# A change of the tile order of batches 0 and 1, of where late weights are decoded, and of how sign and low word are merged

## The chip, the core and the metric

One core of a Trainium2 chip runs the whole program in one launch. The metric is the device time of an execution in microseconds. Before the change three runs took 1471.87 to 1477.98 us, with a median of 1476.96 us.

## What is computed

Attention through 32 packed rows, then a gated layer, then a bilinear one, all in float32:

```python
p_packed = sm_attn(p, k, v)                # 8 batches, 8 heads, 576 rows of 64; 32 packed rows
out = sm_attn(q, p_packed, p_packed)
x = out.transpose(0, 2, 1, 3).reshape(4608, 512)
h = x @ w_in                               # 512 -> 2048
x = (h / (1 + exp(-h))) @ w_out            # 2048 -> 512
out = ((x @ w1) * (x @ w2)) @ w3 @ wo2     # 512 -> 1024 -> 1024 -> 512
```

The weights reach the kernel as float64 words, which it turns into float32 on the chip.

## The kernel before, in words

A matmul of two float32 operands is made of three fp32r matmuls (`mm3`, lines 94 to 97): each operand is split into a high part and a rest (`split`, lines 79, 83 and 88), and high times high, rest times high and high times rest are summed in PSUM.

**Decoding weights.** A float64 tile of 128 x 512 (512 KB) becomes float32 in `Decode` (line 157). ScalarE scales the high words and the low words (line 171 and the one before); VectorE shifts the high word left by three (line 173); the low word is added by GpSimd and the sign bit merged in by VectorE. Without a PSUM bank the add comes first and the merge takes its result (lines 176 and 177); with one, where the high word lies in PSUM, the merge goes into the low word first (line 182) and the add comes last (line 186).

**Stage 1** runs 256 tiles. A tile is one half (f) of a batch (b), 288 rows, and one block m of 128 of the 2048 columns. `emit_h` makes h from a2[b] (the attention weights) and a gate tile of one of 8 slots; `emit_g` applies tanh on ScalarE (line 838) and the product gg on VectorE (line 843), and splits gg on ScalarE and GpSimd; `emit_x2`, three tiles later, multiplies by wo[m] into four PSUM banks, which are evicted to x2_d in DRAM when the last m of the pass is in. The order of the tiles is the list `items`: batch 0 passes half 0 with m 0 to 7, half 1 with m 0 to 7, half 1 with m 8 to 15, half 0 with m 15 to 8, and the first sum of half 0 is stored and added at the end (line 869). From batch 1 on a half passes all 16 m at once. `fetch` (line 781) fills the slots up to 16 tiles ahead from m_d or m01_d, a DMA and a split each.

**The start.** `START` (line 68) is an order written out by hand: what stands before the first bar is emitted ahead of the tiles, and what stands up to the next bar behind each tile. F is a fill, that is a decode of one of 32 tiles of w_in and w_out (order: w_in 0 to 7, w_out 0 to 7, w_in 8 to 15, w_out 8 to 15); L asks for the next raw tile ahead; T is `direct`, a matmul of packed rows of batches 0 and 1 by a w_in tile; W stores a w_in tile to wi_d for later batches; P0, P1, S0, S1 are steps of attention units of batch 0 and 1. Before the change 9 fills stand ahead of the tiles, 7 on tiles 0 to 3, and 16 on tiles 4 to 17; the 16 T stand on tiles 4 to 12 and the 16 W on tiles 6 to 16.

**Three streams** run beside the tiles, paced by `over`, `pack_in` and `paces` (a range of tiles each over which their steps come due, lines 1019 to 1048). Stream x: attention units, one after the other (`chain`): Pack (softmax of the packed rows), four for two batches, and Spread (softmax of the rows, ends with a2), two a batch; the Spreads of batch 1 are due over tiles 15 to 20, the Packs of batches 2 and 3 over 26 to 38, the Spreads of batch 2 over 44 to 62; from tile 209 `prepare_second`, 47 steps due by tile 250, which makes the weights of stage 2: sums of w1 and w2 tiles (`combine`), and the product of w3 and wo2 (`turn`, `product`). Stream y: PackIn, packed rows by w_in for two batches, over 44 to 66. Stream z: `decode_late`, which decodes the 40 tiles of wo2, w3, w1 and w2 over tiles 70 to 205 and stores them to late_d (256 KB each); `prepare_second` reads them back. A planner orders each engine's instructions from this emission order with times of its own.

**Stage 2** (line 1163 on) runs 36 steps of three-part matmuls by the prepared weights.

Of the kernel before, what the change touches and what calls it, by code (L numbers as in the profile page):

```python
# [8 lines left out]
F32 = mybir.dt.float32  # L9
F32R = mybir.dt.float32r  # L10
I32 = mybir.dt.int32
# [11 lines left out]
def attention_swiglu_chain(  # L23
# [39 lines left out]
    EXTRA = 24  # L63
# [69 lines left out]
    late_d = [dram.tile([128, 512], F32, name=f"late_d{n}") for n in range(5 * KM2)]  # L133
# [19 lines left out]
    def bank(name):  # L153
        return ps_f.tile([128, 512], F32, tag="f", name=name)


    class Decode:
# [7 lines left out]
        def __init__(self, raw, z, ps=None):  # L165
            def word(dtype, t):
                return raw.bitcast(dtype).rearrange("p (n t) -> p n t", t=2)[:, :, t]

            high = word(F32, 1) if ps is None else ps
            act_copy(high, word(F32, 1), 2.0**-112)  # L170
            act_copy(word(I32, 0), word(U32, 0), 2.0**-29)
            high = high.bitcast(I32)
            V.tensor_scalar(out=z, in0=high, scalar1=3, scalar2=None, op0=ALU.logical_shift_left)
            if ps is None:
                low = word(I32, 0)
                G.tensor_tensor(out=z, in0=z, in1=low, op=ALU.add)
                V.scalar_tensor_tensor(
                    out=z, in0=high, scalar=-(2**31), in1=z, op0=ALU.bitwise_and, op1=ALU.bitwise_or
                )
            else:  # L180

                V.scalar_tensor_tensor(  # L182
                    out=word(I32, 0), in0=high, scalar=-(2**31), in1=word(I32, 0),
                    op0=ALU.bitwise_and, op1=ALU.bitwise_or,
                )
                G.tensor_tensor(out=z, in0=z, in1=word(I32, 0), op=ALU.add)
            self.z = z.bitcast(F32)
# [109 lines left out]
    class Rows:  # L297
# [6 lines left out]
        def load_rows(self, src):  # L304
            self.x = {}
            src = src[self.b, self.hg]
            for f in self.halves:
                hs = slice(f * HS, (f + 1) * HS)
                if self.early:
                    tag = "gg" if self.lane.second else "sg"  # L310
                    self.x[f] = []
                    for e in range(2):
                        t = g_p.tile([128, HS], F32, tag=tag, name="qT", bufs=2)
# [396 lines left out]
    used_up = [4, 5, 6, 7, 0, 1, 2, 3]  # L710
# [63 lines left out]
    items = [(b, f, m) for b, f in halves[2:] for m in (range(KM) if f == 0 else range(KM - 1, -1, -1))]  # L774

    early_m, late_m = range(KM // 2), range(KM // 2, KM)
    items = [(0, f, m) for f, ms in ((0, early_m), (1, early_m), (1, late_m), (0, late_m[::-1])) for m in ms] + items
    split_at = KM // 2
# [42 lines left out]
    came = []  # L821
    gt = {}
# [13 lines left out]
    def emit_g(i, ps):  # L836
# [5 lines left out]
        gg = g_p.tile([128, HS], F32, tag="gg", name="gg", bufs=2)  # L842
# [7 lines left out]
    def emit_x2(i):  # L850
# [3 lines left out]
        if first_m:  # L854
            acc[b, f] = [ps_acc.tile([128, 512], F32, tag=f"acc{c}", name="ps_x2")[:, 0:HS] for c in range(CD)]
        h_, l_ = gt.pop(i)
        assert ("o", m) in ready
        w = wo[m]
# [3 lines left out]
        if last_m:  # L862
            xs = g_p.tile([128, CD, HS], F32, tag="xs", name="xs", bufs=1)
            rest = (b, f) == (0, 0) and i >= split_at
            if rest:
                move(out=xs, in_=x2_d[b, f])
# [24 lines left out]
    def decode_late():  # L891


        def raw():
            return at.tile([128, 512], U64, tag="raw2", name="raw2", bufs=3)
# [13 lines left out]
        load()  # L909
        yield  # L910
        for n in range(len(late)):
            if n + 2 < len(late):
                load()
            with tc.issue_after(behind["sg"]):
                z = Decode(raws[n], room(n)).z
            store(out=late_d[n], in_=z, age=1)
            yield

    def prepare_second():

        attn.close()
        with tc.tile_pool(name="dec2", bufs=1, side="right") as dp:
            zs = []

            def load():
                n = len(zs)
                zs.append(dp.tile([128, 512], F32, tag="z", name="z", bufs=12))
                move(out=zs[n], in_=late_d[n])
# [49 lines left out]
            ps_w = bank("ps_w34")  # L978
# [48 lines left out]
    over(15, 20, plain([Spread(1, 0), Spread(1, 1)]))  # L1027
# [12 lines left out]
    paces["z"].append((70, at0 + 13, len(late) + 1))  # L1040
# [288 lines left out]
```

## Time and profile before

| what | value |
|---|---|
| median of 3 runs | 1476.96 us |
| the profiled execution's own time | 1475.26 us |
| its span, first to last instruction | 1473.5 us |
| mean granted TensorE clock | 0.987 of full |
| busy: TensorE, its weight loads | 1404.5 us (95%), 1312.4 us (89%) |
| busy: VectorE, ScalarE, GpSimd | 926.1 us (63%), 662.6 us (45%), 601.0 us (41%) |
| moved by DMA | 215.75 MB, mean 146 GB/s |

The span is the time between the first and the last instruction of the profiled execution; its own time is a little longer. Tile 0's tanh stands at 49.5 us, the last tile's at 900.6 us, and stage 2 takes the rest. TensorE is called busy when any matmul is in flight, so the number of matmuls that pass in a stretch tells more than its busy share. A mean over the span mixes stages with different limits; the rows below are by stretch.

### The profile page before, as it was taken

To read this page: it belongs to the slowest core of one execution; us is meant where nothing else is said; L and a number is where in the kernel's file an instruction comes from. 1 tells how busy PE (TensorE), PEld (TensorE's weight loads), DVE (VectorE), ACT (ScalarE), POOL (GpSimd) and SP (SyncE) were. 2 spreads that over 40 slices of the span, in tenths; PEclk is the share of its full clock that TensorE was granted. 3 is DMA by queue.
4 is the path that set the end of the run, shared out by engine and by line. 5 is a ranking of instruction groups with operands and counts; after the bars stand their busy time and mean duration, and the time that the engine had idled before them with its cause. 6 is when DMAs were issued, how large, how long until landed. Compare 5 with 4: busy or idle time off the path is not lost. (4 is left out here: it accounts for less than half of the span.)

```text
span 1473.5 us, 26073 instructions
## 1 busy us (share of the span) xinstructions
PE 1404.5 (95%) x9548; PEld 1312.4 (89%) x9548; DVE 926.1 (63%) x1743; ACT 662.6 (45%) x1442; POOL 601.0 (41%) x606
## 2 busy tenths in 40 slices
PE   7779999799899999999999999999999999999998
PEld 5558999689899998899998899999999999999997
DVE  5976857557876669886888525345454545545453
ACT  5766555556567565575455433223232222323221
POOL 2779655677769966779554231000000000000000
PEclk9999999899999999999999999999999999999999
DMA  8489523676568755476499518610110101101000
GB/s 302 152 276 309 180 82 108 202 227 185 173 182 260 226 174 165 151 235 194 144 303 308 185 63 327 275 58 3 56 49 10 58 1 58 34 25 58 1 30 29
DMA packets 151360, 215.75 MB, mean 146 GB/s; under 512 B 15808, under 2 KB 103104, under 8 KB 150208
## 3 DMA queue, kind: packets, MB, share of 16 engines
q1 hardware_dynamic: 130240, 188.92, 39.8%
q10 hardware_dynamic: 20992, 25.17, 4.9%
q8 instruction: 75, 1.23, 0.3%
q14 instruction: 53, 0.43, 0.1%
HBM read 144.24 MB, written 69.80 MB: 145 GB/s over the span
## 5 line engine op out<-in xcount | busy, mean ns | idle before, releaser
L95 PE MATMUL ps_x<-gh,wo 128*128 128x288 f32 x1024 | 300.8, 298 | 4.0 <-DVE raw L182 3.1
L96 PE MATMUL ps_x<-gh,wo 128*128 128x288 f32 x1024 | 301.4, 298 | 0.0
L97 PE MATMUL ps_x<-gl,wo 128*128 128x288 f32 x1024 | 284.7, 300 | 3.7 <-POOL gl L88 3.3
L88 POOL TENSOR_TENSOR gl<-gg,gh 128x288 fp32r<-128x288 f32 x256 | 232.0, 908 | 94.8 <-ACT gh L79 85.9
L1170 PE MATMUL ps_ab<-xct,w 128*128 128x256 f32 x1728 | 221.2, 284 | 0.0
L1170 PEld LDWEIGHTS ps_ab<-xct,w 128*128 128x128 f32 x1728 | 214.9, 190 | 1.0
L88 POOL TENSOR_TENSOR mq<-mr,mq 128x256 fp32r<-128x256 f32 x176 | 148.9, 847 | 133.5 <-DVE mq L83 68.5
L95 PEld LDWEIGHTS ps_x<-gh,wo 128*128 128x128 f32 x1024 | 193.3, 189 | 7.7 <-DVE raw L182 3.3
L96 PEld LDWEIGHTS ps_x<-gh,wo 128*128 128x128 f32 x1024 | 193.3, 189 | 2.1 <-issue 1.4
L97 PEld LDWEIGHTS ps_x<-gl,wo 128*128 128x128 f32 x1024 | 186.1, 189 | 9.4 <-POOL gl L88 6.4
L79 ACT ACTIVATE gh<-gg 128x288 fp32r<-128x288 f32 x256 | 112.9, 443 | 178.7 <-DVE gg L843 172.3
L95 PE MATMUL ps_h<-a,mq 128*128 128x288 f32 x512 | 159.7, 312 | 24.4 <-DVE gg L843 18.8
L1170 PE MATMUL ps_ab<-xcb,w 128*128 128x256 f32 x1296 | 176.2, 283 | 2.6 <-issue 2.6
L1187 DVE TENSOR_TENSOR r<-p,ps_ab 128x512 f32<-128x512 f32 x72 | 49.2, 684 | 204.0 <-PE ps_ab L1170 203.9
L1170 PEld LDWEIGHTS ps_ab<-xcb,w 128*128 128x128 f32 x1296 | 167.6, 189 | 6.9 <-issue 2.8
L843 DVE SCALAR_TENSOR_TENSOR gg<-sg,ps_h 128x288 f32<-128x288 f32 x256 | 114.0, 446 | 82.4 <-ACT sg L838 37.0
L97 PE MATMUL ps_h<-a,mq 128*128 128x288 f32 x512 | 153.4, 300 | 0.5 <-DVE a L88 0.4
L96 PE MATMUL ps_h<-a,mq 128*128 128x288 f32 x512 | 153.2, 299 | 0.0
L95 PEld LDWEIGHTS ps_h<-a,mq 128*128 128x128 f32 x512 | 97.9, 191 | 37.5 <-DVE gg L843 27.2
L838 ACT ACTIVATE sg<-ps_h 128x288 f32<-128x288 f32 x256 | 102.3, 403 | 56.0 <-PE ps_h L97 31.0
L97 PE MATMUL ps_o<-w,abh 128*128 128x512 f32 x280 | 109.6, 391 | 0.0
L96 PE MATMUL ps_o<-w,abl 128*128 128x512 f32 x280 | 109.5, 391 | 0.0
(177 smaller groups left out, 2582.7 us busy)
## 6 DMA issues: line engine op xcount, KB each, us to landing
mr<-m_d SPq DMA_DIRECT2D x144, 128.0 KB, 3.3
raw<-in_moe_w_dram SPq DMA_DIRECT2D x32, 512.0 KB, 4.4
w_d<-w12s ACTq DMA_DIRECT2D x56, 256.0 KB, 3.9
w<-w_d SPq DMA_DIRECT2D x8, 1792.0 KB, 14.8
wz<-wi_d SPq DMA_DIRECT2D x48, 256.0 KB, 3.8
m_d<-ms SPq DMA_DIRECT2D x96, 128.0 KB, 3.2
raw<-in_moe_w_out_dram SPq DMA_DIRECT2D x21, 512.0 KB, 4.5
late_d<-z ACTq DMA_DIRECT2D x40, 256.0 KB, 4.4
```

Of the source, the lines that this page charges most:

```text
L79: A.activation(out=dst, in_=src, func=ACTF.Copy, scale=mul)
L88: (eng or V).tensor_tensor(out=lo, in0=src, in1=hi.bitcast(F32), op=ALU.subtract)
L95: T.matmul(out=dst, lhsT=wh, rhs=xh, start=start, stop=False)
L96: T.matmul(out=dst, lhsT=wl, rhs=xh, start=False, stop=False)
L97: T.matmul(out=dst, lhsT=wh, rhs=xl, start=False, stop=stop)
L838: ins = A.activation(out=sg, in_=ps, func=ACTF.Tanh, scale=0.5)
L843: ins = V.scalar_tensor_tensor(out=gg, in0=sg, scalar=1.0, in1=ps, op0=ALU.add, op1=ALU.mult)
L1170: T.matmul(out=bank[:, x], lhsT=w[:, wp], rhs=xt[:, kt, xp], start=first and (x, kt, n) == (0, 0, 0), stop=last and (x, kt, n) == (1, 1, 2 ...
L1187: V.tensor_tensor(out=dst, in0=p, in1=q, op=op)
```

## The change

Five things change. The `items` list lets the four halves of batches 0 and 1 pass m 0 to 7, then the four halves pass m 8 to 15; each half's first sum is stored, and loaded again when four tiles of its second pass are in (`part_x2`), where it is added on VectorE. The plan `START` and the due ranges follow: the last 16 fills stand on tiles 8 to 34, eight T on tiles 3 to 6 and eight on tiles 16 to 23, the W on tiles 7 to 10 and 24 to 27; the Spreads of batch 1 are due over tiles 5 to 14; `used_up` takes the tiles in their natural order, and the two raw buffers that lie in a2's place are used by the first 15 fills, not 24. Stream z decodes 20 late tiles (`MID`) over the same tiles 70 to 205; the other 20 are loaded raw and decoded in `prepare_second`, with the high word in a PSUM bank, `ps_dec`. Every decode merges the sign into the low word and adds on GpSimd last. Buffers: gg 4 for 2, raw2 2 for 3, z of `prepare_second` 6 for 12, with three tiles asked for ahead in place of six.

```diff
-    EXTRA = 24
+    EXTRA = 15
+    MID = 20
...
-        "| F F S1 | F S1 | F F S1 | F F | F F T T | F F T T | F W W | F T T W W | F F T T | W W T T "
-        "| F W W T T | F T T | F T T | F W W | F W W | F W W | F W W | F S0 S1 |"
+        "| F L F L S1 | F L S1 | F F S1 | F F T T | T T | T T | T T L | W W L | F L W W | W W | F L W W | | F L "
+        "| | F L | | F T T | T T | F L | | F L | | F T T | T T | W W | L W W | F L W W | W W "
+        "| F L | F L | F L | F L | F L | F L | F | S0 S1 |"
...
-            if ps is None:
-                low = word(I32, 0)
-                G.tensor_tensor(out=z, in0=z, in1=low, op=ALU.add)
-                V.scalar_tensor_tensor(
-                    out=z, in0=high, scalar=-(2**31), in1=z, op0=ALU.bitwise_and, op1=ALU.bitwise_or
-                )
-            else:
...
+            V.scalar_tensor_tensor(
+                out=word(I32, 0), in0=high, scalar=-(2**31), in1=word(I32, 0),
+                op0=ALU.bitwise_and, op1=ALU.bitwise_or,
+            )
+            G.tensor_tensor(out=z, in0=z, in1=word(I32, 0), op=ALU.add)
...
-    used_up = [4, 5, 6, 7, 0, 1, 2, 3]
+    used_up = [0, 1, 2, 3, 4, 5, 6, 7]
...
-    items = [(0, f, m) for f, ms in ((0, early_m), (1, early_m), (1, late_m), (0, late_m[::-1])) for m in ms] + items
-    split_at = KM // 2
+    items = [(b, f, m) for h in range(2) for b, f in halves[:4] for m in range(h * KM // 2, (h + 1) * KM // 2)]
+    items += [(b, f, m) for b, f in halves[4:] for m in (range(KM) if f == 0 else range(KM - 1, -1, -1))]
...
+        rest = (b, f) in part_x2
+        if rest and i == passes[0] + 4:
+            part_x2[b, f] = g_p.tile([128, CD, HS], F32, tag="xs", name="xs", bufs=1)
+            move(out=part_x2[b, f], in_=x2_d[b, f])
...
-            return at.tile([128, 512], U64, tag="raw2", name="raw2", bufs=3)
+            return at.tile([128, 512], U64, tag="raw2", name="raw2", bufs=2)
...
-        for n in range(len(late)):
-            if n + 2 < len(late):
+        for n in range(MID):
+            if n + 1 < MID:
                 load()
...
+            ps_dec, ps_w = bank("ps_dec"), bank("ps_w34")
...
-                zs.append(dp.tile([128, 512], F32, tag="z", name="z", bufs=12))
-                move(out=zs[n], in_=late_d[n])
+                if n < MID:
+                    zs.append(dp.tile([128, 512], F32, tag="z", name="z", bufs=6))
+                    move(out=zs[n], in_=late_d[n])
+                else:
+                    zs.append(dp.tile([128, 512], U64, tag="raw", name="raw", bufs=3))
+                    DMA.dma_start(out=zs[n], in_=late_srcs[n])
...
-                while len(zs) < min(n + 6, len(late)):
+                while len(zs) < min(n + 3, len(late)):
                     load()
                 (kind, i), z = late[n], zs[n]
+                if n >= MID:
+                    z = Decode(z, dp.tile([128, 512], I32, tag="z", name="z", bufs=6), ps_dec).z
...
-    over(15, 20, plain([Spread(1, 0), Spread(1, 1)]))
+    over(5, 14, plain([Spread(1, 0), Spread(1, 1)]))
...
-    paces["z"].append((70, at0 + 13, len(late) + 1))
+    paces["z"].append((70, at0 + 13, MID + 1))
```

## Rows read from the trace of the kernel before

**Rows 1.** Table of stretches: us, busy (x instructions) by engine, clock, DMA share, GB/s.

```profile
63.40:120.60 57.20, 46.83 (x256) 37.44 (x256) 46.71 (x59) 36.40 (x75) 48.38 (x40) 0.93 0.74 246
120.60:183.50 62.90, 61.60 (x426) 57.40 (x425) 48.51 (x93) 36.28 (x84) 50.16 (x53) 1.00 0.74 237
183.50:264.90 81.40, 81.40 (x608) 80.23 (x607) 51.28 (x132) 46.93 (x116) 48.92 (x53) 1.00 0.36 107
264.90:288.70 23.80, 15.14 (x78) 12.02 (x77) 13.14 (x19) 10.09 (x20) 12.66 (x12) 0.87 0.66 194
288.70:725.00 436.30, 418.04 (x2991) 404.50 (x2991) 333.24 (x660) 259.70 (x603) 340.20 (x336) 0.99 0.62 192
725.00:831.00 106.00, 101.48 (x670) 94.06 (x668) 84.57 (x178) 54.06 (x138) 49.41 (x56) 1.00 0.90 293
831.00:886.00 55.00, 54.59 (x341) 50.61 (x342) 15.97 (x36) 18.85 (x43) 17.67 (x23) 1.00 0.20 74
```

**Rows 2.** Stretches again, line 838 alone (tanh on ScalarE, one a tile).

```profile
63.40:120.60 57.20, 4.83 (x12) 0.93 0.74 246
120.60:183.50 62.90, 7.81 (x20) 1.00 0.74 237
```

**Rows 3.** Waits of TensorE in 49.5 to 183.5 us: total, times, longest.

```profile
PE ps_m L668 <- DVE zi L177: 5.5, 1, 5.5
```

**Rows 4.** Timeline, single instructions of the attention units, 163 to 287 us.

```profile
163.83 0.76 DVE L587 STREAM_TRANSPOSE sT<-s 128x576 f32<-128x576 f32 x1
...
167.75 0.38 PE L438 MATMUL ps_t<-ident,e 128*128 128x128 f32 x2
...
235.11 0.38 PE L438 MATMUL ps_t<-ident,e 128*128 128x128 f32 x2
...
284.52 0.78 DVE L587 STREAM_TRANSPOSE sT<-s 128x576 f32<-128x576 f32 x1
...
286.68 0.61 PE L95 MATMUL ps_h<-a,mq 128*128 128x288 f32 x1 [1.29 <-ACT a L79]
```

**Rows 5.** Waits of SP's queue in 215 to 292 us.

```profile
SPq L105 <- POOL v L88: 20.3, 2, 11.7
```

**Rows 6.** Lines 177, 182, 176, 173: ns min/median/max, first and last start; VectorE's wait.

```profile
L177 DVE SCALAR_TENSOR_TENSOR z<-raw,z x49: 680/1277/1785, 72.1 to 720.7; 128x512 int32<-128x512 int32 x49
...
  POOL z L176: 24.8, 20
...
L182 DVE SCALAR_TENSOR_TENSOR raw<-ps_dec,raw x8: 654/679/692, 21.9 to 61.2; 128x512 int32<-128x512 int32 x8
...
L176 POOL TENSOR_TENSOR z<-z,raw x49: 1290/1312/1946, 64.6 to 719.4; 128x512 int32<-128x512 int32 x49
...
L173 DVE TENSOR_SCALAR z<-raw x49: 407/427/1522, 61.8 to 718.6; 128x512 int32<-128x512 int32 x49
...
L173 DVE TENSOR_SCALAR z<-ps_dec x6: 678/680/691, 44.5 to 60.6; 128x512 int32<-128x512 int32 x6
```

**Rows 7.** Waits of TensorE in 288.7 to 725 us.

```profile
PE ps_h L95 <- DVE gg L843: 14.9, 13, 3.6
```

**Rows 8.** DMA issues: count, KB each, median us from issue to landing.

```profile
raw<-in_moe_w_dram SPq DMA_DIRECT2D x32, 512.0 KB, 4.4
...
z<-late_d SPq DMA_DIRECT2D x40, 256.0 KB, 4.5
...
xs<-x_d SPq DMA_DIRECT2D x1, 576.0 KB, 6.3
```

**Rows 9.** Line 869, the adding eviction.

```profile
L869 DVE SCALAR_TENSOR_TENSOR xs<-ps_x,xs x4: 420/452/458, 176.4 to 180.7; 128x288 f32<-128x288 f32 x4
```

**Rows 10.** Tiles late_d and w3T: reloads, and the split of w3T.

```profile
L105 SPq DMA_DIRECT2D z<-late_d x40: 319/332/1179, 726.5 to 808.6; - x40
...
L88 DVE TENSOR_TENSOR w3T<-z,w3T x16: 673/682/1226, 739.1 to 861.7; 128x512 fp32r<-128x512 f32 x16
```

More of the change, by code (lines that the diff above doesn't have):

```diff
@@ L132, in attention_swiglu_chain @@
     w34_d = [dram.tile([128, 2, 512], F32, name=f"w34_d{i}") for i in range(KM2)]
-    late_d = [dram.tile([128, 512], F32, name=f"late_d{n}") for n in range(5 * KM2)]
+    late_d = [dram.tile([128, 512], F32, name=f"late_d{n}") for n in range(MID)]
     x2_d = {(b, f): dram.tile([128, CD, HS], F32, name=f"x2_d{b}_{f}") for b in range(B) for f in range(2)}
@@ L173, in __init__ @@
             V.tensor_scalar(out=z, in0=high, scalar1=3, scalar2=None, op0=ALU.logical_shift_left)
-            if ps is None:
-                low = word(I32, 0)
-                G.tensor_tensor(out=z, in0=z, in1=low, op=ALU.add)
-                V.scalar_tensor_tensor(
-                    out=z, in0=high, scalar=-(2**31), in1=z, op0=ALU.bitwise_and, op1=ALU.bitwise_or
-                )
-            else:
[L182 to L186, printed above, removed]
+            V.scalar_tensor_tensor(
[3 more added lines that the diff above has]
+            G.tensor_tensor(out=z, in0=z, in1=word(I32, 0), op=ALU.add)
             self.z = z.bitcast(F32)
@@ L312, in load_rows @@
                     for e in range(2):
-                        t = g_p.tile([128, HS], F32, tag=tag, name="qT", bufs=2)
+                        t = g_p.tile([128, HS], F32, tag=tag, name="qT", bufs=4 if self.lane.second else 2)
                         move(out=t, in_=src[:, e, hs])
@@ L773, in attention_swiglu_chain @@
     halves = [(b, f) for b in range(B) for f in range(2)]
-    items = [(b, f, m) for b, f in halves[2:] for m in (range(KM) if f == 0 else range(KM - 1, -1, -1))]
-    early_m, late_m = range(KM // 2), range(KM // 2, KM)
-    items = [(0, f, m) for f, ms in ((0, early_m), (1, early_m), (1, late_m), (0, late_m[::-1])) for m in ms] + items
-    split_at = KM // 2
+    items = [(b, f, m) for h in range(2) for b, f in halves[:4] for m in range(h * KM // 2, (h + 1) * KM // 2)]
+    items += [(b, f, m) for b, f in halves[4:] for m in (range(KM) if f == 0 else range(KM - 1, -1, -1))]
     uses = [(b, m) for b, f, m in items]
@@ L821, in attention_swiglu_chain @@
     came = []
+    passes, part_x2 = [0], {}
     gt = {}
@@ L841, in emit_g @@
         behind["sg"] = ins.ins
-        gg = g_p.tile([128, HS], F32, tag="gg", name="gg", bufs=2)
+        gg = g_p.tile([128, HS], F32, tag="gg", name="gg", bufs=4)
         ins = V.scalar_tensor_tensor(out=gg, in0=sg, scalar=1.0, in1=ps, op0=ALU.add, op1=ALU.mult)
@@ L855, in emit_x2 @@
             acc[b, f] = [ps_acc.tile([128, 512], F32, tag=f"acc{c}", name="ps_x2")[:, 0:HS] for c in range(CD)]
+            passes[0] = i
         h_, l_ = gt.pop(i)
         assert ("o", m) in ready
+        rest = (b, f) in part_x2
+        if rest and i == passes[0] + 4:
+            part_x2[b, f] = g_p.tile([128, CD, HS], F32, tag="xs", name="xs", bufs=1)
+            move(out=part_x2[b, f], in_=x2_d[b, f])
         w = wo[m]
@@ L862, in emit_x2 @@
         if last_m:
-            xs = g_p.tile([128, CD, HS], F32, tag="xs", name="xs", bufs=1)
-            rest = (b, f) == (0, 0) and i >= split_at
             if rest:
-                move(out=xs, in_=x2_d[b, f])
+                xs = part_x2.pop((b, f))
+            else:
+                xs = g_p.tile([128, CD, HS], F32, tag="xs", name="xs", bufs=1)
+                if b < 2:
+                    part_x2[b, f] = None
             for c in range(CD):
@@ L908, in decode_late @@
         load()
-        load()
         yield
-        for n in range(len(late)):
-            if n + 2 < len(late):
+        for n in range(MID):
+            if n + 1 < MID:
                 load()
@@ L923, in prepare_second @@
             zs = []
+            ps_dec, ps_w = bank("ps_dec"), bank("ps_w34")
             def load():
                 n = len(zs)
[L927 to L928 removed]
+                if n < MID:
+                    zs.append(dp.tile([128, 512], F32, tag="z", name="z", bufs=6))
+                    move(out=zs[n], in_=late_d[n])
+                else:
+                    zs.append(dp.tile([128, 512], U64, tag="raw", name="raw", bufs=3))
+                    DMA.dma_start(out=zs[n], in_=late_srcs[n])
             o = [dp.tile([128, 2, 512], F32R, name=f"wo2_{j}") for j in range(KM2)]
@@ L976, in step @@
                         combine(i // 2)
-            ps_w = bank("ps_w34")
             w3T = {}
```

## The prediction, made before the changed kernel was run

> **What bounds the kernel now.** I read the table of stretches first: the reader is to see how many matmuls each stretch passes and what the other engines do meanwhile. TensorE is "busy" nearly everywhere, so the count per microsecond is the better gauge. From 183.5 to 264.9 us 608 matmuls pass in 81.4 us, 0.134 us each, with TensorE never idle [rows 1]; I take that as its full pace in the first stage. Against it, 63.4 to 120.6 us holds 256 matmuls, 34.3 us of work in 57.2 us; 120.6 to 183.5 us holds 426, 57.1 us in 62.9 us; 264.9 to 288.7 us holds 78, 10.5 us in 23.8 us [rows 1]. From 831 to 886 us TensorE is busy 54.6 of 55 us [rows 1]: little is left there. So the time to be won lies in 63.4 to 183.5 us (28.7 us), in the hole at 264.9 us (13.3 us) and, thinly spread, in 288.7 to 725 us, where 2991 matmuls (400.8 us) take 436.3 us. The 0.134 us is short for the 512-column and the four-byte matmuls among them, so the true losses are some us smaller.
>
> The count of sigmoid instructions, one a tile, dates the tiles: tiles 4 to 15 take 57.2 us (4.77 each), tiles 16 to 35 take 62.9 us (3.15 each) [rows 2]. The waits of TensorE in 49.5 to 183.5 us are headed by a decode: 5.5 us for a merge into zi [rows 3]. That is the burst of the plan: 23 fills stand on tiles 0 to 17, of which 16 fall after tile 3.
>
> The hole at 264.9 us has another cause. Rows of the timeline show a serial chain of attention units: Spread of batch 1 ends with its transpose at 163.83, the first Pack of batch 2 transposes at 167.75, the fourth at 235.11, so 22.5 us a Pack; the second Spread of batch 2 transposes at 284.52 and TensorE goes on at 286.68, released by ScalarE's a, the split of that transpose [rows 4]. SP's queue meanwhile stands 20.3 us behind a Pack's v split [rows 5].
>
> **The change part by part.**
>
> *Order of tiles and fills (START, items, the Spread of batch 1).* Tiles 0 to 31 need wo 0 to 7 only, so the last 16 fills move from tiles 4 to 17 to tiles 8 to 34, and eight of the sixteen direct products go behind tile 15. The 682 matmuls of 63.4 to 183.5 us are 91.4 us of work [rows 1]. In 120.6 to 183.5 us, where the last of the fills still ran, 9% was lost. At 9% the 120.1 us become 100.4; since 11 fills now meet tiles 18 to 34 and 7 of them the first Packs, I take 14%: 106 us, so 14 us gained by tile 36. Ends: nothing gained (the DMA engines are busy 0.74 of both stretches, and the partial sums add traffic), and 20 us.
>
> *What becomes of it at the hole.* The gain counts only if the chain of units comes forward too. Spread of batch 1 is now due over tiles 5 to 14, not 15 to 20, so the first Pack waits only for its own due tile, 26. Before, that tile stands at about 120.6 + 10 x 3.15 = 152 us; 12 to 14 us earlier is 139. Its transposes would come some 6 us later, at 145, where they stood at 167.75, and 119 us further (286.68 - 167.75) a is ready: 264. Fills beside the first Packs cost it something: per fill 1.3 us of GpSimd and 0.4 + 1.3 us of VectorE [rows 6], 7 fills, of which I put 4 us on the chain: 268. TensorE itself would be there at 264.9 - 14 = 251 and waits, so the hole stays about as long. Start and hole together: 286.7 - 268 = **-18 us**, bounds -3 (the chain hardly moves) and -28 (14 and nearly the whole hole).
>
> *Twenty late decodes out of tiles 70 to 205.* Each takes 0.43 + 1.28 us of VectorE and 1.31 us of GpSimd (medians) [rows 6]: 34 us and 26 us less in a stretch where they are busy 333 and 340 of 436 us [rows 1]. VectorE also stood 24.8 us, 20 times, before a merge until GpSimd's add was done [rows 6]; the merge now comes ahead of the add, so this wait goes, and the reader of z waits for the add instead: for a w_out tile that is ScalarE's split, with tanh and gh queued behind it; for a late tile a store. TensorE's largest wait there is for gg, 14.9 us in 13 waits [rows 7]. VectorE's share falls from 76% to 69%; I take half of that wait: **-8 us**, bounds 0 and -15.
>
> The merge has both inputs in SBUF here and ran 0.68 to 1.79 us; the form with its high word in PSUM stayed within 0.65 to 0.69 us [rows 6]. The Trainium skill (SBUF — State Buffer, Who interferes with whom) says that a VectorE instruction with two SBUF inputs and a GpSimd one that reads SBUF exclude each other for a whole instruction, and that one with a single SBUF input is free of this; the two forms' spreads agree. By that rule the new merge, which no longer starts just behind its own add, meets other GpSimd work as often, nothing of the 24.8 us is won, and the part would be -6 us; it speaks against this piece of the change, not against the sum.
>
> *Partial sums.* Four halves pass twice: three more stores and three more loads of 576 KB than now. A load landed 6.3 us after its issue [rows 8] and is now asked for with four tiles to go into the pass's end half, over 12 us ahead: hidden. The adding evictions are all VectorE's, 0.45 us each [rows 9], four in a row instead of two, so a bank comes free up to 0.9 us later at four passes: +1 us, bounds 0 and +4. Eight refetches of gate tiles fewer: 0, hidden now. The stores of w_in tiles move along SP's queue to tiles 7 to 10 and 24 to 27, the quiet ones: 0. EXTRA 15 takes two of five raw buffers away from fill 15 on; loads land in 4.4 us [rows 8] and fills are mostly two tiles (6 us) apart: 0. If that cover is gone, near tiles 28 to 34 with one fill a tile, each waits up to 1.3 us, off TensorE's path as tile 32 + 3 needs only the first of them.
>
> *Twenty decodes inside prepare_second.* There the high word is in PSUM: 0.68 + 0.68 us of VectorE [rows 6], 27 us, and 26 us of GpSimd. The reads grow from 20 x 256 to 20 x 512 KB, 5.2 MB, 18 us at the 293 GB/s of 725 to 831 us [rows 1], where the DMA engines are 0.90 busy and VectorE 85 of 106 us. Now all late tiles are asked for by 808.6 us and the last w3T split is at 861.7 [rows 10]; behind 831 us VectorE is busy 16 of 55 us and the DMA 0.20 [rows 1]. So 39 us of VectorE and 44 us of DMA are free before stage 2 wants the place, and the work fits behind. What it costs is some more gg lateness: **+3 us**, bounds -1 and +12; if the cover is gone, see the third rival. SP's queue: twenty reloads become raw loads, and with 6 z buffers for 12 and a look-ahead of 3 for 6 a reload can stand there until a combine's parts free its z, some two tiles, with gate refetches behind it; these are asked for up to 16 tiles ahead, so 0. ScalarE's queue loses twenty stores.
>
> **Sum**: -18 - 8 + 1 + 3 = -22. Against the profiled execution's own 1475.3 us that is 1453.3; the median of the runs is 1.7 us above that execution, and I predict 1454.
>
> **The rivals.**
> 1. *The hole eats the start.* If Packs beside fills crawl, a stays near 284 and TensorE only waits longer. For it: the DMA at 0.74 and the SP queue that already stands behind v. Against: three of the four Packs now run with no fill beside them. -3 - 8 + 1 + 3 = -7: 1468.
> 2. *Both give all they can.* Hole closed, gg waits gone: -28 - 15 + 1 + 1 = -41: 1434.
> 3. *The late decodes bind the end.* All twenty share one PSUM bank: ScalarE's copy, the shift and the merge must pass before the next. There are 861.7 - 808.6 - 4.5 (a reload's landing [rows 8]) = 48 us to spare, 2.4 us a decode; shift and merge alone are 1.4 us. With the copy and a place in two busy queues it can be 4.8 us: 96 - 48 = 48 us on the end, net -18 - 8 + 1 + 48 = +23: 1498. It undoes the rest from (48 + 25) / 20 = 3.7 us a decode. Against it: 20 of the 47 steps of prepare_second, due over 41 tiles, carry them, so they spread over some 17 tiles, in the second half of which VectorE idles.
> 4. *The moved work lands where it was.* The emission order is only a start; a planner's sequence per engine could keep the fills early. Then parts one and two are nil: about -4: 1471.
>
> **How the numbers follow.** Forecast 0.50 (own range 1443 to 1463), rival one 0.18, two 0.15, three 0.09, four 0.08. Half a per cent, 7.4 us, is about what a measurement of this kernel can tell from no change. Faster: 0.50 + 0.15 + 0.11 of rival one = 0.76; same 0.07 + 0.08 = 0.15; slower 0.09. The range reaches from rival two, 1434, past rival one and four to 1474, which leaves out rival three and the tails.
>
> **What would show it.** Tile 16 at about 108 us, tile 36 near 170, the first Pack's transposes near 145, TensorE's restart after its long gap near 268; no VectorE wait for GpSimd's add; gg waits in the middle below 10 us; last w3T split before tile 250's place, and stage 2 at full pace. Wrong: the first Pack still near 165, or ps_w matmuls with waits of many us.

## Result: 1.2% faster, and the profile after

The median of four runs is 1457.77 us (1454.91 to 1458.41), of four runs of the kernel before beside them 1476.12. The ratio is 0.9876, with an interval of 0.985 to 0.9902. The profiled execution took 1458.41 us by its own time, with a span of 1456.6, 16.9 us less than before. The forecast was 1454, its range 1434 to 1474.

The total hides what happened, so the first table goes by tiles (the start of tanh of tiles 0, 16, 36, 60, 64, 208 and 255 marks each stretch), in us. Only the last line lies in stage 2.

| stretch | before | after | difference |
|---|---|---|---|
| tiles 0 to 16 | 71.1 | 61.1 | -10.0 |
| 16 to 36 | 62.9 | 67.8 | +4.9 |
| 36 to 60 | 70.2 | 78.1 | +7.9 |
| 60 to 64 (the hole) | 35.0 | 14.9 | -20.1 |
| 64 to 208 (the middle) | 448.7 | 428.5 | -20.2 |
| 208 to 255 (the end) | 163.1 | 181.7 | +18.6 |
| after tile 255's tanh | 572.9 | 574.5 | +1.6 |

Tile 0's tanh itself came 0.4 us later. The same stretches as the table of windows has them, and two inside the end. The columns are: from:to, us, then busy us and instructions of TensorE, its weight loads, VectorE, ScalarE and GpSimd, then granted clock, DMA share, GB/s. After:

```profile
49.90:111.00 61.10, 52.69 (x307) 45.33 (x306) 60.36 (x93) 39.36 (x84) 47.99 (x45) 0.92 0.81 263
111.00:178.80 67.80, 59.38 (x386) 54.33 (x385) 50.17 (x84) 42.21 (x100) 56.82 (x54) 0.95 0.63 202
178.80:256.90 78.10, 78.06 (x582) 76.94 (x581) 49.48 (x132) 45.49 (x109) 44.31 (x47) 1.00 0.52 162
256.90:271.80 14.90, 14.49 (x97) 13.49 (x96) 10.13 (x18) 9.40 (x21) 11.24 (x11) 1.00 0.87 269
271.80:700.30 428.50, 421.76 (x3091) 413.11 (x3091) 299.47 (x637) 244.43 (x571) 301.65 (x321) 1.00 0.54 164
700.30:882.00 181.70, 166.78 (x1044) 152.94 (x1043) 143.16 (x256) 97.80 (x228) 94.88 (x100) 0.97 0.72 235
725.00:831.00 106.00, 92.41 (x551) 82.99 (x550) 98.71 (x169) 63.34 (x148) 64.89 (x65) 0.95 0.81 255
831.00:867.00 36.00, 36.00 (x229) 33.49 (x229) 11.98 (x28) 12.96 (x29) 13.86 (x19) 1.00 0.27 95
```

Before, the five of these tile stretches that [rows 1] does not hold:

```profile
49.50:120.60 71.10, 54.24 (x290) 43.99 (x290) 60.47 (x86) 46.51 (x97) 60.51 (x50) 0.90 0.70 229
183.50:253.70 70.20, 70.20 (x533) 69.61 (x532) 43.15 (x122) 39.43 (x100) 40.64 (x46) 1.00 0.31 91
253.70:288.70 35.00, 26.34 (x153) 22.65 (x152) 21.26 (x30) 17.59 (x36) 20.95 (x19) 0.91 0.68 197
288.70:737.40 448.70, 429.42 (x3073) 415.40 (x3073) 341.92 (x677) 264.32 (x613) 344.68 (x340) 0.99 0.63 193
737.40:900.50 163.10, 159.20 (x1038) 148.26 (x1037) 101.19 (x212) 75.90 (x186) 66.92 (x79) 1.00 0.67 225
```

Three things are to be seen. **The hole is gone**: four tiles pass in 14.9 us with TensorE busy 14.49, where it had 8.7 us idle of 35.0. Of the 153 matmuls that stood there 97 are left, and tiles 36 to 60, where TensorE is never idle before or after, pass 582 in place of 533: their 7.9 us more are work, not loss. **The middle** passes 18 matmuls more in 20.2 us less; 12.5 of these were idle time of TensorE (19.3 down to 6.7), the other 7.7 lay inside its busy time, which [rows 1] could only hint at by the count per microsecond. VectorE fell from 76% to 70%. **The end** is the mirror image: TensorE's idle rises by 11.0 us, its busy time by 7.6, and VectorE goes from 62% to 79% of the stretch. In 725 to 831 us, where [rows 1] had 84.57 us of VectorE and 670 matmuls, it is now 98.71 us and 551 matmuls.

Part of that busy time is TensorE's clock. Before the change 10.6 us of the middle ran at the lower of its two levels (granted 0.50, that is 1.2 GHz in place of 2.4: 288.7 to 292.6 us and the first row below), after it none; of the end, none before and 9.8 us after (the second row, and 775.0 to 778.1 us).

```profile
398.60:405.30 6.70, 5.31 (x22) 5.31 (x23) 4.69 (x16) 2.73 (x6) 4.26 (x6) 0.50 0.63 213
...
747.70:754.40 6.70, 5.81 (x24) 5.81 (x25) 6.06 (x13) 5.16 (x14) 2.59 (x3) 0.50 0.96 334
```

In the second row a matmul passes every 0.28 us, where [rows 1] has 0.134 at full pace. The clock is not what sets the two lengths, though: the late decodes alone, further down, have a granted clock of 0.99 in both stretches and come within 1.1 us of the changed kernel in each.

The count of tanh instructions, as in [rows 2], dates the tiles 16 to 35: 3.15 us each before, 3.39 after.

```profile
49.90:111.00 61.10, 6.42 (x16) 0.92 0.81 263
111.00:178.80 67.80, 7.82 (x20) 0.95 0.63 202
```

The chain of attention units, from the timeline (start, us, engine, line; lines stand some numbers off those of before), answers to [rows 4]: the first Pack's transposes, the fourth's, then the second Spread of batch 2 and the split that makes a.

```profile
154.53 0.38 PE L433 MATMUL ps_t<-ident,e 128*128 128x128 f32 x2
...
221.56 0.38 PE L433 MATMUL ps_t<-ident,e 128*128 128x128 f32 x2
...
266.04 0.78 DVE L582 STREAM_TRANSPOSE sT<-s 128x576 f32<-128x576 f32 x1
...
267.57 0.97 DVE L90 TENSOR_TENSOR a<-sT,a 128x576 fp32r<-128x576 f32 x1 [0.42 <-ACT a L81]
```

Everything stands 13 to 18 us earlier: 167.75 became 154.53, 235.11 became 221.56, 284.52 became 266.04. TensorE reached tile 60 at 256.9, 3.2 us later than before, so chain and TensorE now meet and no gap is left between them.

Waits of VectorE's merge for GpSimd's add (24.8 us, 20 times in [rows 6]) no longer occur, and the wait of TensorE for gg in the middle (14.9 us in [rows 7]) is down to the first line here, from the waits in 271.8 to 700.3 us; the second is from 700.3 to 882 us, where before it was 1.5 us.

```profile
PE ps_h L97 <- DVE gg L837: 4.1, 6, 1.3
...
PE ps_h L97 <- DVE gg L837: 8.6, 8, 1.7
```

### The profile page after: what moved, and what is told of

It is laid out like the page before. It is cut to its first block, busy times and chain, and to the rows that moved or that the text cites. A ratio compares the mean times of both kernels' runs of the same rounds, so it can differ in the third digit from the quotient of the medians.

```text
span 1456.6 us, 25911 instructions
## 1 busy us (share of the span) xinstructions
PE 1399.0 (96%) x9548; PEld 1312.4 (90%) x9548; DVE 924.9 (63%) x1747; ACT 663.8 (46%) x1442; POOL 576.5 (40%) x598
## 3 DMA queue, kind: packets, MB, share of 16 engines
q1 hardware_dynamic: 125920, 186.17, 39.9%
## 4 chain that ended last, share of the span: by engine, by line
PE 67%; DVE 13%; DMA 8%; issue 5%; ACT 4%; POOL 3%; SPq 1%; ACTq 0%; DVEq 0%; POOLq 0%
PE ps_ab L1176 24%; PE ps_x L97 5%; PE ps_x L98 5%; PE ps_x L99 5%; PE ps_o L97 5%; PE ps_o L98 5%; PE ps_o L99 5%; PE ps_h L97 3%; PE ps_h L99 3%; PE ps_h L98 3%; DMA w_d<-w12s 2%; DVE gg L837 1%; DMA mr<-m_d 1%; DVE mq L85 1%; DVE sbd L243 1%
## 5 line engine op out<-in xcount | busy, mean ns | idle before, releaser
L99 PE MATMUL ps_x<-gl,wo 128*128 128x288 f32 x1024 | 289.1, 299 | 0.5 <-POOL gl L90 0.5
L90 POOL TENSOR_TENSOR gl<-gg,gh 128x288 fp32r<-128x288 f32 x256 | 227.9, 893 | 111.5 <-ACT gh L81 96.0
L90 POOL TENSOR_TENSOR mq<-mr,mq 128x256 fp32r<-128x256 f32 x168 | 132.5, 789 | 115.3 <-DVE mq L85 50.1
```

The source lines that it names most:

```text
L90: (eng or V).tensor_tensor(out=lo, in0=src, in1=hi.bitcast(F32), op=ALU.subtract)
L99: T.matmul(out=dst, lhsT=wh, rhs=xl, start=False, stop=stop)
```

## Experiments

The theory after the result had three parts: the order of the tiles brings the attention chain and so tile 64 forward; each late decode that leaves the middle gives it back 1 us; each that arrives in the end takes 0.9 us there, through VectorE. The rivals were that the merge did it, that decodes came too early, that DMA traffic did it, or that the parts are not separable.

**One part alone.** First only the late decodes:

```diff
 (the kernel before, and of the change only:)
+    MID = 20
+            ps_dec, ps_w = bank("ps_dec"), bank("ps_w34")
+                if n >= MID:
+                    z = Decode(z, dp.tile([128, 512], I32, tag="z", name="z", bufs=6), ps_dec).z
...
```

> The kernel before with one part of the change alone: 20 of the 40 late tiles are decoded inside prepare_second (stream z decodes the other 20); order of tiles, START and merges are those of before. Theory (the late weights account for the middle and for the end): tiles 64 to 208, 448.8 us before and 428.5 after the change, take about 432 to 437 us, tiles 208 to 255, 163.1 us before and 181.7 after, about 180 us, so the time is that of before within 5 us, and tile 64 stays near 288 us. Rival (the middle's gain comes from the merges, as VectorE no longer stands for GpSimd's add): the middle stays at 443 to 449 us and the whole is 12 to 18 us slower than before.

Measured 1470.86 us (10 runs), a ratio of 0.9977 (0.9963 to 0.9991). Its two stretches, tiles 64 to 208 and 208 to 255:

```profile
289.30:716.80 427.50, 419.50 (x3057) 410.62 (x3057) 306.75 (x634) 243.62 (x571) 298.07 (x319) 0.99 0.54 164
716.80:897.40 180.60, 164.78 (x1052) 151.59 (x1051) 143.15 (x255) 97.11 (x228) 94.78 (x100) 0.99 0.72 237
```

The move of twenty decodes alone makes -21.2 us in the middle and +17.5 at the end: nearly nothing in sum, and all of what these stretches show in the changed kernel. The old merge is still in it, and so are the two buffers of gg, so neither the merge nor the four buffers freed the middle.

Then only the order (`items`, `START`, the due range of the Spreads, `EXTRA`, `part_x2`), with all 40 late tiles decoded in the middle and the old merge. The four buffers of gg stay in, and the late tiles are loaded with two raw buffers and one tile ahead, where the kernel before had three and two:

> The changed kernel with the late weights as before (all 40 decoded by stream z, 12 z buffers, six asked for ahead; raw2 keeps two buffers, since three don't fit) and with the merges as before. Left: the order of tiles, START, EXTRA and the due tiles of batch 1's Spreads. Theory: tile 64 near 272 us (17 us earlier than before), the middle near the 448.8 us of before, the end near the 163.1 us of before: 15 to 19 us faster than before, about the time of the whole change. Rival (the earlier Spreads and Packs also clear the middle): the middle at 430 to 440 us, so 25 to 35 us faster than before.

Measured 1467.69 us, 0.9955 (0.994 to 0.997): 6 us, where more than twice that was expected. Tile 64 stood at 277.4, 11.3 us earlier than before. Tiles 64 to 208:

```profile
277.40:731.20 453.80, 432.98 (x3100) 418.80 (x3100) 351.66 (x681) 263.84 (x613) 344.80 (x342) 0.99 0.62 193
```

It gives 5.1 us back at once. The row passes 27 matmuls more than before in the same tiles, and 9.7 us more of VectorE in nearly as many instructions (681, from 677), so VectorE's part is mostly the same work made longer. Why is open: the streams that the earlier tile 64 left behind it, the buffers, or chance, since the merge alone, next, differs by nearly as much there. What the four buffers of gg do to the tiles before 64 no run separates from the order.

Then only the merge:

```diff
-            if ps is None:
-                low = word(I32, 0)
-                G.tensor_tensor(out=z, in0=z, in1=low, op=ALU.add)
...
+            G.tensor_tensor(out=z, in0=z, in1=word(I32, 0), op=ALU.add)
```

> The kernel before with the new merge alone: the sign goes into the low word, GpSimd's add comes last. Theory: within 4 us of before; VectorE's 24.8 us of waits for the add vanish, but TensorE's waits for gg in the middle fall by less than 4 us. Rival (the merges make the middle): tiles 64 to 208 in 438 us or less, 10 us or more faster than before.

Measured 1477.34 us (10 runs), 1.0013 (1.0001 to 1.0025). In tiles 64 to 208 no wait of VectorE's merge for GpSimd's add is left, and yet TensorE waits as before (14.9 us in [rows 7]). The wait has changed sides: now GpSimd's add stands for the merge.

```profile
POOL z L178 <- DVE raw L174: 14.7, 14, 2.7
...
PE ps_h L95 <- DVE gg L835: 13.8, 12, 2.9
```

A wait of 24.8 us (18.1 of it in these tiles) on an engine with a quarter of its time to spare was worth nothing by itself; the tiles took 452.7 us, 4.0 more than before.

By medians the three parts alone give -3.3, -6.4 and +3.2 us, together -6.5, and the whole gives -18.3. They are **not additive**. To see where they meet, the changed kernel was run with the old merge alone put back:

> The changed kernel with the merge of before where there is no PSUM bank (add first, merge last). Theory (by the difference of the order alone to the whole change, the new merge is worth some 5 us in the first 36 tiles and nothing later, where only 20 decodes are left): tile 64 at 276 to 279 us instead of 271.9, the middle within 3 us of 428.5, 3 to 7 us slower than the changed kernel. Rival (the merge is worth nothing anywhere, as alone on the kernel before): within 2 us of the changed kernel, tile 64 within 2 us.

Measured 1460.37 us (3 runs), 0.9908 (0.988 to 0.9936), 2.6 above the changed kernel, less than the intervals settle. Its profile says where: tile 64 at 276.4 and tiles 16 to 36 in 71.3 us, the very figure of the order alone, against 67.8 to 68.0 in most of the runs with both parts.

```profile
112.00:183.30 71.30, 59.26 (x387) 54.80 (x387) 53.24 (x88) 42.57 (x100) 57.82 (x55) 0.93 0.63 204
```

So the merge is worth about 3.5 us in these tiles of the changed kernel; alone on the kernel before, it left them at 62.7 us (62.9). That it helps only where the order has put fills beside Packs is likely, not tested. Most of the 12 us between the sum of the parts and the whole lies in the middle: the 5 us that the order lost there and the 4 of the merge are not lost in the whole kernel, whose middle (428.5) is as short as that of the late decodes alone (427.5). That VectorE's lower load, 70%, makes the room for it is argued from these rows, not shown.

**What makes the hole close.** In the changed kernel the Packs were put later:

```diff
-    over(26, 38, [Pack(2...
+    over(36, 44, [Pack(2...
```

> The changed kernel with the four Packs of batches 2 and 3 due over tiles 36 to 44 instead of 26 to 38, behind the last fill. Theory (the chain Pack, Pack, Pack, Pack, Spread, Spread sets tile 64, and Packs beside fills cost tiles 16 to 36 the time): tile 36 at 168 to 173 us instead of 178.9, but the first Pack's transposes near 180 instead of 154.5 us, and tile 64 at 285 to 298 us instead of 271.9, so the hole is back and the whole 10 to 25 us slower than the changed kernel. Rival (the fills alone cost tiles 16 to 36, and tile 64 waits for TensorE's own work): tile 36 near 179 us and tile 64 within 5 us of 271.9.

One run: 1463.49 us. Tiles 16 to 36, and tiles 60 to 64:

```profile
110.90:173.10 62.20, 54.70 (x364) 49.89 (x363) 42.15 (x66) 38.66 (x89) 54.34 (x52) 0.97 0.69 225
...
245.30:282.10 36.80, 29.68 (x174) 24.84 (x173) 29.03 (x49) 20.85 (x41) 23.52 (x21) 0.98 0.65 188
```

TensorE stood at tile 36 5.7 us earlier (173.2) and at tile 64 10.2 us later (282.1), with the hole back at 36.8 us. So the chain of units sets tile 64 when it is late, and the Packs beside fills cost tiles 16 to 36 some 5.5 us; this run shows both. One part of the expectation missed: the first Pack's transposes still stood at 156.0, not near 180. Its next step did move (the transpose of its packed rows started at 182.4 us, 164.4 in the changed kernel), and the second, third and fourth Pack came later with it. Why its head did not move stays open.

**What a decode costs at the end.** First the decode was left out but its traffic kept: the 20 raw loads stay, 20 loads of 256 KB are added, and the products of these tiles use weights that are not theirs.

```diff
-                if n >= MID:
-                    z = Decode(z, dp.tile([128, 512], I32, tag="z", name="z", bufs=6), ps_dec).z
...
+                    zs[n] = dp.tile([128, 512], F32, tag="z", name="z", bufs=6)
+                    move(out=zs[n], in_=late_d[n - MID])
```

> The changed kernel, where prepare_second loads the last 20 late tiles raw (512 KB each) but doesn't decode them: it also loads 20 other decoded tiles (256 KB each) and goes on with these, so two products use the wrong weights and the DMA moves 5 MB more than in the changed kernel. Theory (VectorE's 27 us of shifts and merges, beside what they do to the rest of VectorE's work, bind the end, 98.7 of 106 us busy): tiles 208 to 255 fall from 181.7 to about 165 us. Rival (the raw loads bind, the DMA being 0.81 to 0.96 busy there): they stay at 178 us or more.

One run: 1440.33 us, the end 162.0 us, no longer than before the change, though the DMA share is higher than in any other run (the column before the last):

```profile
725.00:831.00 106.00, 105.63 (x677) 98.46 (x676) 72.04 (x155) 52.63 (x134) 43.33 (x53) 1.00 0.92 308
```

TensorE is busy 105.63 of 106 us beside DMA engines at 0.92. The traffic is not the price; the engines' work for the decode is.

Then ten of the twenty back to the middle (`MID = 30`):

> The changed kernel with 30 late tiles decoded by stream z and 10 in prepare_second. Theory (each decode in the middle costs what VectorE is short of there, each one at the end likewise): the middle (tiles 64 to 208) about 436 to 440 us, the end (208 to 255) about 170 to 173 us, the whole within 5 us of the changed kernel. Rival (the costs set in only past a load that the middle bears): with 30 the middle stays near 430 us and the end falls by 9 us, so the whole is 6 to 9 us faster than the changed kernel.

Measured 1456.43 us, 0.9892 (0.9872 to 0.9912): the middle 437.8 us (+9.3), the end 170.2 (-11.5). That is 0.93 and 1.15 us a decode, nearly the same price at both places, and the sum stays.

Then all twenty at the end, but held back so that the place of gg in the queue comes first:

```diff
+                    with tc.issue_after(behind["gg"]):
+                        z = Decode(z, dp.tile([128, 512], I32, tag="z", name="z", bufs=6), ps_dec).z
```

> The changed kernel, where each decode in prepare_second may be ordered only behind the newest gg of its emission, so that it doesn't run ahead of its due tile. Theory (the planner takes the decodes too early, at 725 to 822 us, while VectorE has some 20 us free behind 831 us): the end falls from 181.7 to 170 to 176 us, 6 to 11 us faster than the changed kernel. Rival (the decodes are where their consumers need them, and VectorE's sum of work is what counts): no change within 4 us.

Measured 1455.48 us, 0.9887 (0.987 to 0.9903). The decodes' adds moved from 728 to 822 us to 759 to 847, and the end is still 181.7 us. My theory that they only came too early falls; its loss moved with them:

```profile
725.00:831.00 106.00, 97.94 (x600) 89.44 (x599) 81.97 (x154) 61.94 (x143) 61.22 (x63) 0.97 0.72 229
831.00:885.00 54.00, 48.45 (x310) 45.36 (x309) 34.02 (x64) 24.46 (x57) 23.86 (x26) 0.94 0.62 219
```

The first 106 us passed 49 matmuls more than in the changed kernel, and the 54 us behind them are no longer the quiet place that they were.

**VectorE's load taken down in other ways.** The high split of the gate tiles was put on ScalarE:

```diff
-                split_hi(slots[:, far, :, 0], t, True)
+                split_hi(slots[:, far, :, 0], t)
```

> The changed kernel with the high part of each gate tile made by ScalarE instead of VectorE (168 casts of 256 columns). Theory (VectorE binds the end and the stretch of tiles 16 to 36, and its SBUF copies also stand behind GpSimd): VectorE's busy time in 725 to 831 us falls from 98.7 to below 92 us, the end to 170 to 176 us, tile 36 comes 2 to 6 us earlier, the whole 6 to 15 us faster than the changed kernel. Rival (ScalarE's queue, with tanh and gh in it, becomes the place of the wait): the same or slower than the changed kernel.

Measured 1463.75 us, 0.9946 (0.9929 to 0.9963), 6 us slower than the changed kernel. VectorE's busy time in 725 to 831 us fell to 94.7 us and the end to 178.2, but the middle grew to 434.5. The wait of VectorE for the tanh, in 276 to 711 us, shows the new bound; the same wait of the changed kernel in 272 to 700 us was 26.5 us in 35 times.

```profile
DVE gg L837 <- ACT sg L832: 108.4, 72, 5.0
```

ScalarE makes the tanh for gg, and with the casts in its queue gg waits for the tanh four times as long.

Next, part of the rests of the w1 and w2 sums went to GpSimd:

```diff
-                    split(t[:, :, 0], t[:, :, 1], src.rearrange("p (j n) -> p j n", j=2))
+                    split_lo(t[:, :, 1], src, t[:, :, 0], G if j > 2 else V)
```

> The changed kernel, where the rests of the four parts of each combine that come from sums (32 subtractions of 256 columns) are made by GpSimd, not VectorE. Theory (VectorE's work binds the end; GpSimd is busy 65 of 106 us there): VectorE's busy time in 725 to 831 us falls by 15 us or more and the end from 181.7 to 168 to 174 us. Rival (GpSimd's adds already stand in the way of VectorE's instructions with two SBUF inputs and of gl; more work there makes that worse): the end at 180 us or more.

Measured 1456.93 us, 0.9887 (0.9851 to 0.9922); the end was 178.6 us, 3 us shorter for 5.8 us less of VectorE (92.91 of 106, from 98.71; 15 had been expected) and 21.5 us more of GpSimd (86.40, from 64.89):

```profile
725.00:831.00 106.00, 92.59 (x571) 83.90 (x571) 92.91 (x147) 65.50 (x153) 86.40 (x94) 0.98 0.82 261
```

GpSimd went from 61% to 82% of this stretch and the end did not grow, so GpSimd's load is not what binds it. Three runs took work off VectorE in this stretch without moving a decode elsewhere, and each shortened the end: 26.7 us off for 19.7 (the undecoded run, with the decodes' work on ScalarE and GpSimd gone too), 5.8 for 3.1 (this one), and 4.0 for 3.5 (the one before, where ScalarE did more). That speaks for VectorE as the engine through which a decode costs TensorE its time.

**Other places for the decodes.** Ten of them (`MID = 30`) over tiles 38 to 62, where TensorE was at full pace beside a VectorE 63% busy:

```diff
-    paces["z"].append((70, at0 + 13, MID + 1))
+    paces["z"] += [(38, 62, 10), (70, at0 + 13, MID - 9)]
```

> The changed kernel with 30 late tiles in stream z, ten of them due over tiles 38 to 62 and twenty over 70 to 205 as now, so that prepare_second decodes ten. Theory (tiles 36 to 60, where TensorE loses 0.7 of 78 us and VectorE is busy 49.5 us, can carry ten decodes for next to nothing, while ten fewer at the end give back 11 us): the middle stays at 428 to 431 us, the end near 170 us, tile 64 within 3 us of 271.9; 8 to 12 us faster than the changed kernel, about 1447 us. Rival (the decodes there delay the chain of Packs and Spreads, and the hole comes back): tile 64 later by 6 us or more, and the whole within 5 us of the changed kernel.

Measured 1453.68 us (4 runs), 0.9869 (0.9837 to 0.99). The middle (422.3) and the end (169.5) win 18 us, but the chain pays: the hole opens to 24.5 us and tile 64 comes at 287.2, 15.3 us later.

```profile
178.90:257.00 78.10, 75.98 (x557) 73.27 (x555) 60.22 (x141) 49.25 (x119) 49.47 (x47) 1.00 0.60 192
...
262.70:287.20 24.50, 20.96 (x136) 18.83 (x135) 17.49 (x28) 13.47 (x28) 20.06 (x19) 1.00 0.91 284
```

It has the lowest median of all kernels that decode every tile, but its interval overlaps the changed kernel's; better is not shown. Last, eight decodes at the seam of middle and end, tiles just before 209, where from 612.3 to 700.4 us the changed kernel had VectorE 59.2 of 88.1 us busy and TensorE all of it (`MID = 28`):

```diff
+    paces["z"] += [(70, at0 + 13, MID - 7), (at0 - 8, at0 + 14, 8)]
```

> The changed kernel with 28 late tiles in stream z: twenty over tiles 70 to 205 as now and eight more over tiles 184 to 206, so that prepare_second decodes twelve. Theory (a decode costs nothing where TensorE loses nothing and no chain sets a date: tiles 176 to 208, 612.3 to 700.4 us, where TensorE is never idle, VectorE is busy 59 of 88 us and GpSimd 60): the middle takes 429 to 432 us, the end 171 to 175 us, tile 64 within 3 us of 271.9; 4 to 9 us faster than the changed kernel. Rival (a decode costs 0.9 us in the middle wherever it stands, as with 30 spread evenly): the middle at 435 us or more, the whole within 3 us of the changed kernel.

Measured 1457.39 us (5 runs), 0.9888 (0.9872 to 0.9903): the middle 436.3 (+7.8), the end 176.5 (-5.2), that is 0.98 and 0.65 us a decode. The seam had no free room either:

```profile
612.00:700.00 88.00, 84.11 (x591) 81.26 (x591) 71.38 (x115) 52.21 (x114) 71.27 (x72) 0.98 0.65 195
```

VectorE went from 67% to 81% there and TensorE lost 3.9 us at once.

## Why the forecast was right, and where its terms were not

**Start and hole: forecast -18, measured -16.8.** Tile 64's tanh came at 271.9 in place of 288.7, and TensorE's first matmul on a started at 267.8, where 268 stood. The reason held in the main: the Packs move forward and a comes out of their chain, which sets tile 64 when it is late (the late Packs show it). But the waypoints show another road. Tile 16 near 108 came at 111.1. *Tile 36 near 170* failed: 178.9. The prediction took 14% of loss for tiles 18 to 34 with 11 fills and the first Packs; the stretch from 16 to 36 took 4.9 us longer than before, and by the run with late Packs the Packs beside fills alone are 5.5. *The first Pack near 145* failed as well: 154.5. Its due tile, 26, came at 141.7 for 139, and the transposes followed 12.8 us behind, not 6. That the date of a was right nonetheless is because the chain ran from the first Pack's transposes to a in 113 us, not in the 119 taken plus 4 for the fills: two misses that cancel. And *TensorE waits there, so the hole stays about as long* was wrong: TensorE reached tile 60 3.2 us later than before, not 14 earlier, and found its work. Rival one, that the hole eats the start, is refuted by the row of 256.9 to 271.8 us.

**Middle: forecast -8, measured -20.2, outside its bounds of 0 and -15.** The step that failed is *I take half of that wait*: the price was read off the row of the longest wait, 14.9 us [rows 7]. The wait did shrink, to 4.1. But VectorE's lateness also cost where no single wait is listed: TensorE's idle fell by 12.5 us and its busy time by 7.7 at more matmuls, part of that by the clock. The count of [rows 1] had 35 us to lose in that stretch, and a bound from it would have held. The right row was that one.

**Merge.** The forecast weighed two readings: part of the wait for the add is won, or, by the rule of the Trainium skill that it cites, nothing. VectorE's wait vanished, GpSimd's took its place, and the merge alone won nothing, so the second reading was the better one. The two forms in the changed kernel (ns min/median/max, first and last start):

```profile
L177 DVE SCALAR_TENSOR_TENSOR raw<-raw x38: 622/1124/1789, 58.3 to 675.9; 128x512 int32<-128x512 int32 x38
L177 DVE SCALAR_TENSOR_TENSOR raw<-ps_dec,raw x28: 623/676/693, 20.7 to 821.7; 128x512 int32<-128x512 int32 x28
```

With both inputs in SBUF it still takes up to 1.79 us, with one in PSUM never over 0.69. That agrees with the rule of the Trainium skill (SBUF — State Buffer, Who interferes with whom) that a VectorE instruction with two SBUF inputs and a GpSimd one that reads SBUF exclude each other. The runs do not separate it from the other reason, that a wait on an engine with time to spare costs nothing.

**Partial sums: forecast +1, bounds 0 and 4.** TensorE waited 0.2 us, once, for one of the 16 adding evictions (199.4 to 283.4 us), and 2.4 us, twice, for the plain evictions of the first sums in 49.9 to 178.8 us, where before the change such waits came to 0.6. Right in size, then, but not through the adding; and the loads were hidden: no wait of VectorE for xs is listed.

**End: forecast +3, measured +18.6, outside its bounds of -1 and +12.** The step that failed is *39 us of VectorE and 44 us of DMA are free before stage 2 wants the place, and the work fits behind*. It does fit, and stage 2 starts on time: the last w3T split stands at 843.3 us, before tile 250's place, and 1.6 us is all that is lost after tile 255. But the work did not go behind. Its last merge started at 821.7 us, in the stretch where VectorE was already 85 of 106 us busy; there it lost gg's place. The held-back run shows that it would not have helped to go behind: what fills the quiet place makes it as dense as the other. The DMA side of the step was right (0.92 beside a full TensorE).

The two terms missed by 12 and 16 us with opposite signs, and so the sum came out. They are one error: a decode was priced by waits at one place and by free time at the other, and costs about 1 us of TensorE at both (0.93 and 1.15 by the run with ten moved back). That the sum came within 4 us of the median is therefore luck, though its largest term, the first, rests on a chain that the runs bear out. (Its last step is 1 us short: 1453.3 and 1.7 make 1455.) Twenty decodes that change place then give little, as the late decodes alone show, and the gain of the whole is that of the order and of the room that the middle has for it.

**Rivals two to four.** The hole did close and nearly all the gg wait went, as rival two had it, but the end took 19 us. Rival three priced the end's loss through the one PSUM bank, on the last product; the twenty merges started 5.0 us apart, from 726.1 to 821.7 us, near its 4.8, but some 80 us sooner than it assumed, and ScalarE waited for a merge to free the bank only 2.7 us, in 3 waits. Rival four fell with the first row: tile 16 moved by 10 us.

**What stays open.** What stretches VectorE's other work at the end. Its busy time from tile 208 to 255 rose by 42 us for 27 us of decodes; most of the other 15 us are two kinds of instruction of unchanged number, the 32 casts of gate tiles (12.3 us before, 17.1 after) and the 56 rests of w1 and w2 parts (31.9 and 39.9). Without the decodes, in the undecoded run, they took 9.9 and 30.5 us, so it is the decodes that stretch them. Of the rests, those of the sums went from a median of 426 ns (before, 742 to 831 us) to this:

```profile
L90 DVE TENSOR_TENSOR w12s<-sums,w12s x27: 409/536/1531, 729.8 to 830.9; 128x256 fp32r<-128x256 f32 x27
```

That GpSimd's adds are what stretches them is argued from the spread of these durations alone, not shown: no run had the adds without VectorE's share of the decode. Open too are the share of gg's four buffers in the first 64 tiles, and why the first Pack's head did not move in the run with late Packs. A version that is clearly faster than the changed kernel was not found.

## What to carry to other kernels

Price work that moves from one dense stretch to another by what it costs TensorE at both ends, from the matmuls per microsecond of each stretch, not from the longest listed wait at one end and from idle time at the other: here both terms were wrong by more than 10 us and only cancelled. Before asking what an engine's wait is worth, see whether that engine has time to spare; a wait of 24.8 us on VectorE was worth nothing alone. And parts of a change that compete for one engine must be tried together as well as alone: three parts that gave 6.5 us one by one gave 18.

## What the runs showed that was not expected

**TensorE loses long before VectorE is full.** With VectorE 63% busy (178.8 to 256.9 us of the changed kernel) TensorE had no idle time, nor with 67% (612.3 to 700.4). With 77% (the ten early decodes, 178.9 to 257) it was idle for 2.1 of 78 us, with 80% (725 to 831 us before the change [rows 1]) for 4.5 of 106, with 81% (the seam) for 3.9 of 88, with 93% (725 to 831 us after) for 13.6 of 106. I had counted all of VectorE's idle time as free, and above three quarters none of these stretches bears that out. But the share alone does not decide, and no limit can be read off these rows: the held-back run lost 8.1 of 106 us at 77%, tiles 16 to 36 of the changed kernel, with fills and Packs, 8.4 of 67.8 at 74%, and its middle still 6.7 of 428.5 at 70%.

**Four tiny casts can take 4 us.** Four casts of 32x64 elements stand in one row of 4.11 us on VectorE (0.34, 1.77, 0.72 and 1.20 us), while GpSimd is busy without a break; TensorE then waited 2.9 us for the gg behind them. From the timeline of the changed kernel:

```profile
164.72 4.11 DVE L243 CAST sbd<-pkT 32x64 fp32r<-32x64 f32 x4
...
169.46 0.43 DVE L837 SCALAR_TENSOR_TENSOR gg<-sg,ps_h 128x288 f32<-128x288 f32 x1
...
169.95 0.40 PE L97 MATMUL ps_h<-a,mq 128*128 128x288 f32 x1 [2.91 <-DVE gg L837]
```

The shortest of these casts in the same kernel took 176 ns, the median 266 and the longest 2058. GpSimd has subtractions of 0.78 to 1.83 us one behind the other from 164.97 to 168.77 us. That they hold the casts up is likely: a cast is among the operations of which the Trainium skill (SBUF — State Buffer, Who interferes with whom) says that they can, under conditions on their operands, take the port pair that VectorE shares with GpSimd, and the 4 us agree with it; no run took the subtractions away.
